# One queue for the key weights, one for x: the first loads of an attention and gMLP block on one core

## The chip, the core and the metric

The kernel runs on one core of a Trainium2 chip. The core has five engines with an instruction stream each: TensorE (PE in the profile), VectorE (DVE), ScalarE (ACT), GpSimd (POOL) and SyncE (SP). SyncE computes nothing here; it issues transfers. ScalarE can issue transfers too, and in this kernel it issues a few. The metric is the time of one execution on the device in microseconds, lower is better; a comparison takes the median of several runs.

## The reference, cut to what matters

Two blocks in a row on x (2048 tokens by 512 features, bf16), each behind a layer norm and with a residual:

```python
x = A_x
h  = x + A(layernorm(x), wqkv, wo)           # linear attention, 32 heads of 16
h2 = h + B(layernorm(h), w_in, w_sp, b_sp, w_out)

# A: phi(t) = where(t > 0, t + 1, exp(t)) + 1e-6
q, k, v = split(x @ wqkv)
kv  = einsum('bhsd,bhse->bhde', phi(k), v);  z = phi(k).sum(s)
out = (phi(q) @ kv) / (phi(q) @ z + 1e-6) @ wo

# B: z1, z2 = halves of gelu(x @ w_in), each 896 wide
g   = w_sp @ layernorm(z2) + b_sp            # w_sp is 2048 x 2048
out = (z1 * g) @ w_out
```

## The kernel before, in words

Tokens are handled in 16 tiles of 128 rows, numbered 0 to 15, and in 4 token groups (tg) of 512. The work runs in these stages, which overlap.

**Loads.** `first_load` and `load_x` issue the first transfers in a fixed chain for each queue. x0 to x3 are one tile each; x4, x6, ... x14 are two tiles each. A load with `behind` waits, on its engine, for another load to land.

**Key units** (`k_unit(n)`, tiles n and n+1). For each tile: statistics (`stats`: a 676 ns `bn_stats`, L511, and a short `bn_aggr`, L512, on VectorE; for the tiles in `ACTS`, two ScalarE passes with accumulation and four GpSimd operations); 1/sqrt(var + eps) (`rstd_act` by Ln and Exp on ScalarE for tiles 0, 2 and 3, `rstd` by pow on GpSimd for others); the norm to `xn` (L556 on VectorE up to tile 5, an Identity on ScalarE from tile 6); the transpose to `xnT` (on TensorE, L570, with a copy by ScalarE up to tile 5; by a DMA transpose on SyncE's queue, named xt6 to xt15, L435, from tile 6); four matmuls with the key weights (L402, `psum<-wqkv,xnT`); `phi` to `pk`; and four matmuls that add pk^T xn into four PSUM banks (L655). Those banks hold a 512 x 512 sum ct, from which the kv product is made later with the value weights `wv` (L720).

**phi** is an Exp on ScalarE from PSUM to `e`, a minimum and an addition on VectorE (L582), and then one of two forms: on VectorE alone a max of (psum + 1 + eps) and e (L587), or, with `split`, an Identity with bias on ScalarE from PSUM to the destination and a max of that and e on VectorE (L585).

**Query units** make phi(q) in `pqT`, from the weights `wq`. **z** is summed with a matmul of ones (L676). Then the kv product (L720), masked to blocks on VectorE (`kvm`), is multiplied by `wo` to `m`; the denominators of a token group (L751) become 1/den by Ln and Exp on ScalarE (`r`, `rcp`), and four copies on SyncE's queue spread that to 128 rows (`r<-rcp`, L742), with which VectorE divides `pqT` (L764).

**h.** For each tile four matmuls `psum<-m,pqT`, and VectorE adds x (L776). Three PSUM banks are used in turn. ScalarE squares h with accumulation (`sh`), GpSimd makes mean and 1/std, VectorE the norm `hn` (L556), and SyncE's queue transposes it to `hnT` (L435, ht0 to ht15).

**The gMLP half.** z2 of a tile is eight matmuls (L802, L805, "psum<-win,hnT"), z1 of a group four (L402). Then w_sp (transposed by DMA on SyncE's queue, `dma_t`, in blocks of 128 columns of the result, whole or as two halves), the gating, and the output product. TensorE's part of this lasts from 64.85 us to the end.

**What sets the order.** Every operation is recorded by `add` with the regions it reads and writes; `ORDER`, a packed list, gives the order of all 961 operations. `schedule` unpacks it and `emit` splits it by engine and puts a semaphore wait in front of an operation that needs another engine or a DMA. Engines run their lists strictly in order, so an operation that waits holds all behind it. A transfer that SyncE issues stands in SyncE's list like any operation. `soft` entries and `cost`, `lat` figures serve the planning only.

**The head's queues before.** SyncE: x0, x2, half of the key weights (wk0), x4, x6 (both behind x2's landing), x8, x10, x12, x14 (behind wk0's), wq, one whole block of w_sp, then xt7, xt6 and on. ScalarE: x1, x3, the other half of the key weights (wk2), then the load of its Exp/Ln table.

Of the kernel before, what the change touches and what calls it, by code (L numbers as in the profile page):

```python
# [8 lines left out]
ACT = mybir.ActivationFunctionType  # L9
ALU = mybir.AluOpType  # L10

P = 128
GRAN = 16
EARLY = 1
SEM_NS = 45.0
ORDER = "c-jTQ17HvU00h8Cwq47%ZQHhO+qGrewr$(CZ5wwH5gAbt9Wf9Su@D<^5Eu2800D@ED2Rr5$b~$}jl4*LqyUHz2nE3iiC_qhWJrz_NQp#9j8w>n{3w9JNQ(-ngvO|hifD@XNQl%(gMui6bjW~0NROh(gp4SL;;4eE$c!dvhAgOttSEtOsEO>Tj&A6I?kI_#D23)|fpBPrmgt4v=!-tcfm*16wy2FdXpPdSi+UJ`GAN7sXn-*oi}6^7B{+=bSc-PYiE=294rqh+XoyA_fPol{e&~-u=!i}@g3dUILzsYxn1sn#foYh6Ay|pf2#+ubi&cn#)i{b{IDz9BieU)ENCaUNMq>@uVLGOw3%X(^W?%v4<1|iU78YVH*5eGG;uKz@fg0)sp5qy2V-AL61U6tJ7GW`VU^_NpGqzwZ=3x)^VkdTCH_qWK_F+E`U@Nxa3a;WjF5n_A;U+HQ8gAh_Zr~N(;5FXjHtypN?&2OEA~+u)1Vi#2BJdF+G7{h8F`nQjKHvvF;uk*QAHLu-zTqprBPPMH49!ps!&o$9Gb*DoGNUja<1-H9G91J6H)1dqQ!@`UGdlA!3-hx8(=aX5F+DRdBQvoaOS2ZqeEfr~EJ*P$$}kwSF*|cGCkwGWb1{GkSeQjvl*L$=3Au#z*pj)~gSA<lCE13Fn3xr~m}Oa?OIe4l*qXiBmVH=}l~|co*p6$smJQgDjaZfK*^@Qcm`&J=eVLTWS%RgQgvq#t$(4dlnUc-9hbgp-TbWvEG@MgdjoUbaBiWA~*pZ#sp99#L138Gxxt%+>f-5<d={22=)L1pSjx(4+d%2HY*p1EDg4LN)sgzl1704hC<zRMaR}SM4Hc=L(Q$~$qCQai^o?%vHQ+DN0PUTiE<y9W#S3VU`K^0aZ713E9VR02z2^CXml~fs(S1Fa%9UkQ|-sKg(;Z>H?6TW2y&EkF@;6bkE25#hNj^S92<4*44A&%#4&f#3H;yg~^ah~9OF63cO;wEn9J>KU7KIBQB;yb?Q2cF}3Uf@OU=4r0xHD2c>HdQk<R|~aND^2DCPUIq1RAp7tA3o(X{$&+a)fawcHHBAeB~u%<RXep;2X#~@bygR3RRn!waD`A!g;Xtl<a6HOO+MlazT_>w;wS!NL|x`<J|+}NRAhbU5B}sY-e!CyP!xqyXh~rdRbgcXD4~8ckrFG3s;h>gD~3KZreZ0!!YP`PDvshRnBr-G`e?9ftFC6Kj%I3zhN_+hs;_2ixVmYIrfQJ7tG{|^l~!w-rYle*HCMybQzO(*qclz%G+MnBr16@ddFrkC8lzd7sC8PPC0eMpO5(Aaqyw6xrCOuOTBh~dsLfiWE!wJs+NPvltP@(U?b@Xk+N71*p}jh+L)xvK+Nb?GqCGmQ<4Wk0I;GP(qeMQY#LnfjI;RvquM4`QD@y5$itl8;rcb)A54x<Yx}&?grJK5^+`g{|O6>#=@JBt;L#6U#J<|(4(Nm@MXT8=drE_{e*B8CiS7q=!z125;*AFFk7XQ*uW%O_T6a7bjmEXZ^!*XbcabAaX2#0lehjSWda#m+{HWzR~M{q<(avn!@WJh-t7jkw-a|{=DKF4t^$8-+obP*SIF_&>!7k3HQbA88kBR6&vH*hmIbxD_ULr-!GH+OlrbSw9A8~1h}w{}IBb|qK#1o!hq_jP{{a67kkdk^#=5AiTp@nBbVIoEInS95jObS>9*M|bu{*Ku8UcMnhTR8MmUZ}Mgj^(+r}Cy(?DPxlsg@np|*kViPsvpvsqJl6}n$V)um3%%G&J<g-u)nmQfqrA+kywYpD*6SSG!F@yV+|!}F)$jF2x7E#KyxJ=~-s`==+q~U7ywkh<AMVe{ZU"


class _Op:
# [233 lines left out]
def bass_sequential_preLN__linear_attn_block__mixer_gmlp__prompt_kernel(  # L253
# [11 lines left out]
    _, S, D = A_x.shape  # L265
    F = B_w_in.shape[1]
    FH = F // 2
    H = 32
# [9 lines left out]
    g = _Prog(nc)  # L278
# [41 lines left out]
    x = g.sbuf("x", o_x, [NT, D], BF16)  # L320
    h = g.sbuf("h", o_x, [NT, D], BF16)
    xn = g.sbuf("xn", o_xn, [NT, D], BF16)
    wqkv = g.sbuf("wqkv", o_wqkv, [KD, 3 * D], BF16)
# [4 lines left out]
    pk = g.sbuf("pk", o_pk, [NT, D], BF16)  # L328
# [146 lines left out]
    def first_load(eng, dst, src, nm, lat, behind=None):  # L475
        q = queue[eng]
        op = load(eng, dst, src, nm, lat)
        op.bias = 1e6
        if q:
            op.soft.add(q[-1].i)  # L480
        if behind is not None:
            op.deps.add(behind.i)
        q.append(op)
        return op

    def load_x(eng, n, w, lat, behind=None):
        return first_load(eng, x[:, n:n + w, :], x_d[n * P:(n + w) * P, :], f"x{n}", lat, behind)

    x0 = load_x("SP", 0, 1, 2150)
    load_x("ACT", 1, 1, 2250)  # L490
    x2 = load_x("SP", 2, 1, 2500)
    load_x("ACT", 3, 1, 2500)
    wk = [first_load(eng, wqkv[:, c:c + 2, D:2 * D], A_wqkv[c * P:(c + 2) * P, D:2 * D], f"wk{c}", 3500)
          for eng, c in (("SP", 0), ("ACT", 2))]
    for n, lat, behind in ((4, 2000, x2), (6, 2200, x2), (8, 1900, wk[0]), (10, 2100, wk[0]), (12, 2300, wk[0]),
                           (14, 2500, wk[0])):
        load_x("SP", n, 2, lat, behind)
    first_load("SP", wqkv[:, :, 0:D], A_wqkv[:, 0:D], "wq", 3400)
    exp_table = g.add("ACT", lambda ac: ac.preload_act_table_set("natural_log_exp_and_others"), [], [], cost=1300)
    exp_table.soft.add(queue["ACT"][-1].i)  # L500
    exps = []
# [12 lines left out]
    def rstd(s, r, n, w, col, neg, sign=1.0):  # L514

        rr, ss = r[:, n:n + w, :], s[:, n:n + w, :]
        pool(lambda p: p.tensor_scalar(rr[:, :, 1:2], ss[:, :, col + 1:col + 2], sign, EPS_LN, op0=ALU.mult,
                                       op1=ALU.add), [ss[:, :, col + 1:col + 2]], [rr], 230)
        pool(lambda p: p.tensor_tensor(rr[:, :, 0:1], rr[:, :, 1:2],  # L519
                                       expo[:, 0:w].rearrange("p (a b) -> p a b", b=1), ALU.pow), [rr, expo], [rr],  # L520
             620 + 120 * (w - 1))
        if neg:
            for i in range(n, n + w):
                pool(lambda p, i=i: p.tensor_scalar(r[:, i, 2:3], s[:, i, col:col + 1], r[:, i, 0:1], -1.0,
                                                    op0=ALU.mult, op1=ALU.mult), [r[:, i, :], s[:, i, :]], [r[:, i, :]], 240)

    def rstd_act(s, r, n, w, col):
        rr, ve = r[:, n:n + w, :], s[:, n:n + w, col + 1:col + 2]
        act_exp(rr[:, :, 1:2], ve, ACT.Ln, 80, bias=epst[:, 1:2], extra=[epst[:, 1:2]])
        act_exp(rr[:, :, 0:1], rr[:, :, 1:2], ACT.Exp, 80, scale=-0.5)  # L530
# [22 lines left out]
    def norm(eng, dst, src, s, r, n, col, w):  # L553
        mean, rst, nmr = s[:, n, col:col + 1], r[:, n, 0:1], r[:, n, 2:3]
        if eng == "DVE":
            return dve(lambda v: v.tensor_scalar(dst, src, mean, rst, op0=ALU.subtract, op1=ALU.mult), [src, mean, rst],  # L556
                [dst], w + 460, acc=4)
        elif eng == "ACT":
            act(dst, src, ACT.Identity, w, bias=nmr, scale=rst, extra=[nmr, rst])
        else:  # L560
            pool(lambda p: p.tensor_scalar(dst, src, rst, nmr, op0=ALU.mult, op1=ALU.add), [src, nmr, rst], [dst],
                 200 + 1.5 * w)
# [43 lines left out]
    def next_pair():  # L606
        pc[0] += 1
        return PAIRS[pc[0] % 2]

    CB, first_xt, second = [4, 5, 6, 7], None, None  # L610
    HEAD, SINGLE = 6, 4
    ACTS = (1,)
    QSPLIT, KSPLIT, CACT = (6, 7), (), 2


    def k_unit(n):
        nonlocal first_xt, second
        b = next_pair()
        for i in (n, n + 1):
            if i in ACTS:  # L620
                s = st[0][:, i, :]
                act(sh_t[0], x[:, i, :], ACT.Identity, D, accum=s[:, 0:1])
                act(sh_t[1], x[:, i, :], ACT.Square, D, scale=D ** -0.5, accum=s[:, 1:2])
                moments(s, 6, D)
                rpow(s[:, 7:8], rs[0][:, i, 0:1])
            else:
                op = stats(x, 0, i)
                if i == 0:
                    second = warmup(16, 60, op)
                if n == 0:  # L630
                    rstd_act(st[0], rs[0], i, 1, 6)
        if n == 2:
            rstd_act(st[0], rs[0], n, 2, 6)
        elif n:
            rstd(st[0], rs[0], n, 2, 6, n >= HEAD)
        for i in (n, n + 1):
            norm("DVE" if n < HEAD else "ACT", xn[:, i, :], x[:, i, :], st[0], rs[0], i, 6, D)
            if n < HEAD:
                pe_transposes(xn[:, i, :], b + i % 2, xnT, i, second)
            else:  # L640
                g.last = dma_t(xnT[:, :, i * P:(i + 1) * P], xn[:, i, :], f"xt{i}")
                if i == HEAD:
                    first_xt = g.last
        for i in (n, n + 1):
            matmuls(bank(b + i % 2), [(xnT[:, c, i * P:(i + 1) * P], wqkv[:, c, D:2 * D]) for c in range(KD)])
        if n < SINGLE:
            for i in (n, n + 1):
                phi(pk[:, i:i + 1, :], b + i % 2, 1)
        else:
            phi(pk[:, n:n + 2, :], b, 2, n in KSPLIT)  # L650

        def fn(pe, i):
            inst = None
            for c in range(KD):
                inst = pe.matmul(bank(CB[c]), lhsT=xn[:, i, c * P:(c + 1) * P], rhs=pk[:, i, :],  # L655
                                 start=i == 0, stop=i == NT - 1)
            return inst
        for i in (n, n + 1):
            PE(lambda pe, i=i: fn(pe, i), [xn[:, i, :], pk[:, i, :]], [bank(b) for b in CB], KD * 216)
# [67 lines left out]
    for c in range(KD):  # L727
        b = CB[1 - c % 2]
# [100 lines left out]
    k = 0  # L829
# [190 lines left out]
```

## Time and profile before

| | us |
|---|---|
| median of 4 runs | 233.42 (232.74 to 233.94) |
| the profiled execution | 233.36 |
| its span in the profile | 231.6 |
| TensorE busy | 224.8 |
| VectorE busy | 161.3 |
| ScalarE busy | 104.7 |
| GpSimd busy | 44.9 |

The granted clock of TensorE is 1.0 in the whole profile. The profile is of one execution; times in it count from the start of the span, and 1.76 us of the execution lie outside it. A line of the timeline gives the start, the length, the engine, the source line, the operation with output and input, the number of instructions merged into it, and, in brackets, how long the engine sat idle before it and what ended that. A matmul's own length (379 ns for 512 columns) includes its way through the array; successive ones start 216 ns apart. A line of DMA issues ends with the time from issue to landing. The chain of waits is followed back from the last instruction, and its shares are 89% TensorE, 4% DMA and 3% ScalarE.

### The profile page before, as it was taken

Reading aid. Unit: us, or ns where it says so; the run is one execution under the profiler, and the core shown is the slowest. Engines: PE = TensorE matmul, PEld = TensorE weight load, DVE = VectorE, ACT = ScalarE, POOL = GpSimd, SP = SyncE. Lnnn points to the kernel's source line nnn. Section 1 sums busy time; section 2 is a strip of 40 time slices with the busy share of each in tenths; the row PEclk is TensorE's granted clock in tenths of the full one; section 3 lists DMA queues with packets and bytes.
Section 4 is the critical chain, followed back from the end, with each engine's and each line's share of the span. In section 5 each row is a group of like instructions: output and inputs, shape, how many; then the busy total and the mean of one; then the engine's idle time right before and its main releaser. Section 6 shows DMA issues by size and latency. Waiting matters only on the chain.

```text
span 231.6 us, 3254 instructions
## 1 busy us (share of the span) xinstructions
PE 224.8 (97%) x1203; PEld 110.5 (48%) x1203; DVE 161.3 (70%) x323; ACT 104.7 (45%) x193; POOL 44.9 (19%) x134
## 2 busy tenths in 40 slices
PE   7898999999999999999999999999999999999995
PEld 7433444453444443454544444444455555555452
DVE  3998656646986650237489989979795566785485
ACT  5794754399889876679862010101021211123010
POOL 2436300000467608033771000000000000000000
PEclk9999999999999999999999999999999999999999
DMA  5893359927457537959999700000000000020025
GB/s 185 260 214 69 67 143 274 343 64 178 96 110 135 115 71 134 190 112 175 181 231 204 159 3 0 0 0 0 3 0 1 0 3 0 21 71 3 0 81 191
DMA packets 58864, 23.68 MB, mean 102 GB/s; under 512 B 48480, under 2 KB 58720, under 8 KB 58848
## 3 DMA queue, kind: packets, MB, share of 16 engines
q1 hardware_dynamic: 58144, 22.88, 44.5%
q10 hardware_dynamic: 704, 0.59, 0.7%
q8 instruction: 9, 0.15, 0.2%
q14 instruction: 7, 0.06, 0.1%
HBM read 7.47 MB, written 2.10 MB: 41 GB/s over the span
## 4 chain that ended last, share of the span: by engine, by line
PE 89%; DMA 4%; ACT 3%; DVE 1%; issue 1%
PE psum L402 72%; PE psum L802 6%; PE psum L655 5%; PE psum L805 4%; DMA xnT<-xn 2%; DMA hnT<-hn 1%; DMA x<-in_A_x_dram 1%; DVE st L511 1%; ACT sh L421 1%; ACT xn L421 1%; PE psum L570 1%; ACT e L421 1%; ACT xnT L421 0%; PE psum L751 0%; PE psum L676 0%
## 5 line engine op out<-in xcount | busy, mean ns | idle before, releaser
L421 ACT ACTIVATE psum<-psum 128x256 f32<-128x256 f32 (+1 forms) x33 | 14.3, 445 | 90.8 <-PE psum L402 63.1
L402 PE MATMUL psum<-wsp,z 128*128 128x512 bf16 x208 | 47.7, 379 | 0.0
L402 PEld LDWEIGHTS psum<-wsp,z 128*128 128x128 bf16 x208 | 20.4, 98 | 22.9
L402 PE MATMUL psum<-hnT,win 128*128 128x512 bf16 x112 | 26.1, 379 | 0.0
L421 ACT ACTIVATE e<-psum 128x1024 bf16<-128x1024 f32 (+1 forms) x18 | 16.7, 926 | 15.0 <-PE psum L402 14.4
L402 PE MATMUL psum<-t,s 128*128 128x512 bf16 x96 | 22.4, 379 | 0.0
L421 ACT ACTIVATE z1T<-psum 128x512 bf16<-128x512 f32 x28 | 16.6, 594 | 4.9 <-PE psum L402 4.8
L802 PE MATMUL psum<-win,hnT 128*128 128x512 bf16 x64 | 16.4, 379 | 0.5 <-DMA hnT<-hn 0.5
L402 PE MATMUL psum<-wout,z1T 128*128 128x256 bf16 (+1 forms) x83 | 16.7, 315 | 0.0
L402 PEld LDWEIGHTS psum<-hnT,win 128*128 128x128 bf16 x112 | 10.0, 98 | 13.2 <-ACT z1T L421 3.8
L402 PE MATMUL psum<-wqkv,xnT 128*128 128x512 bf16 x64 | 15.0, 379 | 1.2 <-DMA xnT<-xn 1.2
L421 ACT ACTIVATE z<-psum 128x896 bf16<-128x896 f32 x16 | 14.6, 910 | 2.9 <-PE psum L805 2.8
L402 PE MATMUL psum<-xnT,wqkv 128*128 128x512 bf16 x64 | 15.6, 379 | 0.0
L655 PE MATMUL psum<-pk,xn 128*128 128x512 bf16 x64 | 15.3, 379 | 0.0
L402 PE MATMUL psum<-m,pqT 128*128 128x512 bf16 x64 | 14.8, 379 | 0.2 <-DVE h L776 0.2
L402 PEld LDWEIGHTS psum<-t,s 128*128 128x128 bf16 x96 | 9.4, 98 | 10.3
L776 DVE SCALAR_TENSOR_TENSOR h<-psum,x 128x512 bf16<-128x512 f32 x16 | 10.8, 687 | 4.8 <-PE psum L402 4.8
L582 DVE TENSOR_SCALAR e<-e 128x1024 bf16<-128x1024 bf16 (+1 forms) x18 | 7.0, 391 | 9.2 <-ACT e L421 9.0
L805 PE MATMUL psum<-win,hnT 128*128 128x384 bf16 x64 | 13.0, 326 | 0.0
L924 DVE TENSOR_TENSOR u<-psum,bsp 128x512 bf16<-128x512 f32 x16 | 11.0, 687 | 2.8 <-PE psum L402 2.7
L556 DVE TENSOR_SCALAR z<-z,st,rs 128x896 bf16<-128x896 bf16 x16 | 7.2, 494 | 7.3 <-POOL rs L519 7.3
L511 DVE BATCH_NORM_STATS2 st<-x 128x6 f32<-128x512 bf16 x15 | 9.7, 676 | 3.5 <-DMA x<-in_A_x_dram 3.5
(113 smaller groups left out, 347.5 us busy)
## 6 DMA issues: line engine op xcount, KB each, us to landing
r<-rcp SPq DMA_DIRECT2D x16, 128.0 KB, 2.7
out_dram<-h SPq DMA_DIRECT2D x15, 128.0 KB, 1.8
win<-in_B_w_in_dram SPq DMA_DIRECT2D x2, 896.0 KB, 6.7
x<-in_A_x_dram SPq DMA_DIRECT2D x6, 256.0 KB, 3.4
wqkv<-in_A_wqkv_dram SPq DMA_DIRECT2D x2, 512.0 KB, 5.1
wout<-in_B_w_out_dram SPq DMA_DIRECT2D x1, 896.0 KB, 6.2
wo<-in_A_wo_dram SPq DMA_DIRECT2D x1, 512.0 KB, 8.4
bsp<-in_B_b_sp_dram SPq DMA_DIRECT2D x1, 512.0 KB, 5.7
```

Of the source, the lines that this page charges most:

```text
L402: inst = pe.matmul(out_ap, lhsT=a, rhs=b, start=start and i == 0, stop=stop and i == len(pairs) - 1, **kw)
L421: return g.add("ACT", lambda ac: ac.activation(out_ap, in_ap, func, **kw), [in_ap, *extra], [out_ap] + ([accum] if accum is not None else []),
L511: dve(lambda v: v.bn_stats(s[:, 0:6], src[:, n, :]), [src[:, n, :]], [s[:, 0:6]], D)
L556: return dve(lambda v: v.tensor_scalar(dst, src, mean, rst, op0=ALU.subtract, op1=ALU.mult), [src, mean, rst], [dst], w + 460, acc=4)
L570: inst = pe.transpose(tv[:, c * P:(c + 1) * P], src[:, c * P:(c + 1) * P], ident)
L582: dve(lambda v: v.tensor_scalar(e, e, 1.0, EPS_PHI, op0=ALU.min, op1=ALU.add), [e], [e], w * GW, acc=4)
L655: inst = pe.matmul(bank(CB[c]), lhsT=xn[:, i, c * P:(c + 1) * P], rhs=pk[:, i, :], start=i == 0, stop=i == NT - 1)
L776: dve(lambda v, n=n, b=b, s=s: v.scalar_tensor_tensor(h[:, n, :], bank(b), 1.0, x[:, n, :], op0=ALU.mult, op1=ALU.add, accum_out=s[:, 0:1] ...
L802: pe.matmul(bank(b), lhsT=hnT[:, c, n * P:(n + 1) * P], rhs=win2[:, c, 0:GW], start=c == 0, stop=c == KD - 1)
L805: inst = pe.matmul(bank(b + 1, F2), lhsT=hnT[:, c, n * P:(n + 1) * P], rhs=win2[:, c, GW:FH], start=c == 0, stop=c == KD - 1)
L924: dve(lambda v: v.tensor_tensor(t, bank(b), add, ALU.add), [bank(b), add], [t], GW, ps=True)
```

## The change

The first loads are dealt out anew. ScalarE's queue carries one load only, all four row blocks of the key weights (512 KB) in one transfer. SyncE's queue carries every x load: x0, x1, x2, x3, then x4 and x6 behind x2's landing, the rest behind that of the key weights, then wq. `EARLY = 0` takes away the whole block of w_sp that was transposed at the head; that block is now transposed in two halves, later. `ACTS = ()` gives tile 1's statistics to VectorE and its 1/std to ScalarE's Ln and Exp. `KSPLIT = (0, 1)` makes phi of key tiles 0 and 1 the split form, with an Identity on ScalarE. `ORDER` is new as a whole: the order of nearly every engine's list differs from before. `ND` and `LEAD` are empty and do nothing.

In the new order TensorE transposes tiles 0 to 2, does the key matmuls of tile 0, transposes tile 3, and goes on with the key matmuls of tiles 1 to 3; VectorE does the statistics of tiles 0 to 3 before any norm. SyncE's list is x0 to x14, wq, nine xnT transposes, wout, the last xnT transpose, win2, half a block of w_sp, wo, wv, win1, the r copies of groups 0 and 1, the other half block, the r copies of group 2, ht0, ht1 and on; before, wv stood ahead of the last xnT transpose, wout and two half blocks of w_sp followed, then win1, win2 and wo, and no w_sp stood among the r copies of groups 0 to 2.

```diff
-EARLY = 1
+EARLY = 0
...
-    x0 = load_x("SP", 0, 1, 2150)
-    load_x("ACT", 1, 1, 2250)
-    x2 = load_x("SP", 2, 1, 2500)
-    load_x("ACT", 3, 1, 2500)
-    wk = [first_load(eng, wqkv[:, c:c + 2, D:2 * D], A_wqkv[c * P:(c + 2) * P, D:2 * D], f"wk{c}", 3500)
-          for eng, c in (("SP", 0), ("ACT", 2))]
-    for n, lat, behind in ((4, 2000, x2), (6, 2200, x2), (8, 1900, wk[0]), (10, 2100, wk[0]), (12, 2300, wk[0]),
-                           (14, 2500, wk[0])):
+    wk = first_load("ACT", wqkv[:, :, D:2 * D], A_wqkv[:, D:2 * D], "wk", 4300)
+    load_x("SP", 0, 1, 2250)
+    load_x("SP", 1, 1, 2350)
+    x2 = load_x("SP", 2, 1, 2550)
+    load_x("SP", 3, 1, 2750)
+    for n, lat, behind in ((4, 1750, x2), (6, 1950, x2), (8, 2000, wk), (10, 2200, wk), (12, 2400, wk), (14, 2600, wk)):
         load_x("SP", n, 2, lat, behind)
...
-    ACTS = (1,)
-    QSPLIT, KSPLIT, CACT = (6, 7), (), 2
+    ACTS, ND, LEAD, lead = (), (), 0, []
+    QSPLIT, KSPLIT, CACT = (6, 7), (0, 1), 2
...
-                phi(pk[:, i:i + 1, :], b + i % 2, 1)
+                phi(pk[:, i:i + 1, :], b + i % 2, 1, i in KSPLIT)
```

## The prediction

> **What bounds the kernel now.** I read the shares first, then the chain of work that ended last, then TensorE's idle times in the timeline, then SyncE's issues and the landings.
>
> Busy time by engine, from the page:
>
> ```profile
> PE 224.8 (97%) x1203; PEld 110.5 (48%) x1203; DVE 161.3 (70%) x323; ACT 104.7 (45%) x193; POOL 44.9 (19%) x134
> ```
>
> TensorE (PE) is busy for all but 6.8 us. The change neither adds nor removes a matmul, so only those 6.8 us can move. The timeline of TensorE (start, length, what, idle before) names the idle time that matters:
>
> ```profile
> 14.42 2.75 PE L655 MATMUL psum<-pk,xn 128*128 128x512 bf16 x12
> 18.33 1.90 PE L402 MATMUL psum<-wqkv,xnT 128*128 128x512 bf16 x8 [1.16 <-DMA xnT<-xn]
> ...
> 55.06 0.39 PE L402 MATMUL psum<-wo,kvm 128*128 128x512 bf16 x1 [0.31 <-ACT m L421]
> ...
> 63.02 1.04 PE L402 MATMUL psum<-m,pqT 128*128 128x512 bf16 x4 [0.23 <-DVE h L776]
> 63.99 0.40 PE L751 MATMUL psum<-pqT,zc 128*32 128x512 bf16 x4
> 64.85 1.04 PE L802 MATMUL psum<-win,hnT 128*128 128x512 bf16 x4 [0.46 <-DMA hnT<-hn]
> ```
>
> After 64.85 no idle of TensorE is listed to the end. So the last 231.60 - 64.85 = 166.75 us are fixed work, and **the sum is about one number: when the first L802 matmul starts.** The chain of waits says what leads there:
>
> ```profile
> 14.36 3.92 DMA xnT<-xn
> 18.28 0.04 issue
> 18.33 1.90 PE psum L402 x8
> ...
> 61.33 3.47 DMA hnT<-hn
> 64.80 0.05 issue
> 64.85 1.04 PE psum L802 x4
> ```
>
> SyncE's issues say why the transpose that ends at 18.28 began only at 14.36:
>
> ```profile
> 8.99 5.31 SPq L435 DMA_TRANSPOSE wsp<-in_B_w_sp_dram  x1
> 14.36 5.54 SPq L435 DMA_TRANSPOSE xnT<-xn  x4
> ```
>
> The w_sp transpose holds the queue for 5.31 us. ScalarE had finished the first tile that the queue was to transpose (12.20 + 0.80) at 13.0.
>
> **The change part by part.** *The w_sp transpose leaves the head.* The first xnT transpose can issue as soon as ScalarE writes its tile, and its landing falls from 3.9 us to the 2.5 of the median row. If nothing else changed, TensorE would go on at 17.0 (12 matmuls of 0.216 from 14.42) instead of 18.33, a gain of 1.3 at most. What is late next is TensorE's own work before it, so the loads must be counted.
>
> *The loads.* Before, x0 and x1 go out at 0.79 and 0.80 on two queues, x2 and x3 behind them, and one half of the key weights on each. These rows carry the landings (count, KB each, us to landing):
>
> ```profile
> x<-in_A_x_dram SPq DMA_DIRECT2D x2, 128.0 KB, 2.7
> x<-in_A_x_dram ACTq DMA_DIRECT2D x2, 128.0 KB, 2.9
> wqkv<-in_A_wqkv_dram SPq DMA_DIRECT2D x1, 256.0 KB, 4.8
> wqkv<-in_A_wqkv_dram ACTq DMA_DIRECT2D x1, 256.0 KB, 5.0
> ```
>
> x0 keeps 3.47. x1 takes the place of x2 as SyncE's second load: 1.25 + 2.8 = 4.05. x2 and x3 are third and fourth, and no row shows that. From below: the second tile lands 0.56 after the first, so 4.6 and 5.2. From above: SyncE's third and fourth 128 KB were the weight half, 1.71 + 4.8 = 6.5, so 5.3 and 6.5. I take 4.8 and 5.5, nearer to the spacing, as x rows lie next to each other in memory and the weights' do not. The whole weight load lands between those ends, at 6.0 to 6.7, ahead of its use.
>
> At one place a rule speaks against this part. In 2.5 to 3.5 us the two queues' recorded packets are 217 and 179, near equal. The Trainium skill, "DMA: Bandwidth & Descriptors", "Issuing engines are not separate DMA queues" and "Queues, rings and completion order", says that both queues run on the same 16 engines, taking turns, and that a second issuer saves only issue time. By it the four tiles would advance only as fast as the weights beside them and x3 would land with the weights: the second rival's 233.5, where the rows' spacing gives 232.8.
>
> VectorE then does stats of four tiles (tile 1 moves here from ScalarE, which drops two ACTIVATEs of 0.63; GpSimd drops four operations): x1 4.08 to 4.7, x2 4.85 to 5.5, x3 5.55 to 6.2, aggregates to 6.4 (before 5.79). The pair's Ln and Exp take 0.6 to 7.05; xn0 and xn1 fill 6.4 to 7.05; xn2 and xn3 start at 7.07 and 7.4. Transposes of tiles 0 to 2 run 6.86 to 7.85 and the first key matmul starts at **7.95, before 7.75.** Four groups (0.86 each) and tile 3's transposes (0.32) end at 11.7.
>
> *phi of tiles 0 and 1.* ScalarE gains two Identity passes, which the trace lacks at this size: half of the 128x1024 row (1.11) is 0.55, the 128x512 copy 0.60. VectorE's 0.67 (PSUM source) becomes a max at 0.42 at most (128x512 bf16 row). ScalarE holds them: from 7.3 to 11.8 it does 4 copies, 2 exps and 2 Identities, 8 x 0.5. Were that cover gone, the copy of tile 3's transpose would be late and TensorE would wait 0.5. For VectorE it is 0.25 less, twice, ahead of the two later tiles' norms.
>
> *To the 18.33 line.* Transposes of tiles 4 and 5 end at 12.4 (before 12.7), then four pk and two key groups, 6 x 0.86, to **17.6**. xn7 is ready at 13.5, its transpose lands at 13.55 + 2.5 to 2.9 = 16.4, the next 1.26 later: both in time. So 17.6 for 18.33, a gain of 0.7.
>
> *The middle.* The order is written anew. The last pk groups end at 46.3 (before 47.03). ScalarE's chain from ct to the last m is the same 13 instructions; with one 0.5 wait for TensorE it ends at 55.7, and h starts at 55.75 (before 56.58). But h of tile 0 on VectorE now stands behind the minimum of the last query exp: exp 55.7 to 56.6, minimum to 57.05, h 57.1 to 57.8 (before 57.65 to 58.3). Square, GpSimd's four operations and the norm take what they took (57.65 to 61.3), so hn0 ends at 60.75; SyncE is free then (r from 57.85, four at 0.62). It issues at 60.78 and the landing takes its 3.47: 64.25, so **L802 starts at 64.3, before 64.85.** TensorE itself is ready at 63.45: from 55.75 eight h groups of 0.86, one L751 group of 0.33, and a 0.5 wait, since tile 4's products need tg 1's division, which VectorE does between h tiles.
>
> *w_sp elsewhere.* The head's block is now two halves, one behind win2 and one between the r copies of groups 1 and 2; the other fourteen follow among and behind the hnT transposes. Issue is 1.31 to 2.77 each. Nine of them stand behind the last hnT, near 97.5: at 1.35 they are issued by 110 and land within 6, before TensorE's first use at 120.15. wv stands behind wout, win2, one half and wo: about 3.1 MB from 31.5 at the 247 GB/s that those loads made before (4.3 MB, 31.05 to 48.5) is 44.2, needed at 48.5. Cost nothing; the cover is 4 us of TensorE's q and z groups, and without it TensorE would wait at the kv product.
>
> **Sum:** 64.85 - 64.3 = 0.55, so 233.36 (the profiled execution: span 231.60 and 1.76 around it) - 0.55 = 232.8. The median of the four runs, 233.42, is 0.06 above it, so the forecast for a median is 232.8 too.
>
> **Rivals.** *Both stalls shrink fully.* If hnT lands in the 2.5 us of its median row, L802 starts at 63.45, where TensorE is ready: 1.4 gained, 232.0; with x3 at 5.2 (0.3 more) 231.7. For it: the 3.47 had r copies around it. Against: they still are.
>
> *The change does not do what it says.* x3 lands with the weights at 6.5: everything to 17.6 moves by 0.7 to 18.3, and since the h chain hangs on the same start, L802 is at 65.0: 233.5, no change.
>
> *Slower: the w_sp half between the r copies.* It is issued at 55.5 and all r copies of group 2 and hnT stand behind it on SyncE's queue. Its landing is 3.7 us in one row, 6.5 in a row behind wout, 8.9 in the head row (a whole one):
>
> ```profile
> wsp<-in_B_w_sp_dram SPq DMA_TRANSPOSE x1, 3.7
> ...
> wsp<-in_B_w_sp_dram SPq DMA_TRANSPOSE x1, 6.5
> ...
> wsp<-in_B_w_sp_dram SPq DMA_TRANSPOSE x1, 8.9
> ```
>
> At 3.7 it is gone by 59.2. From 7 us on it decides: hnT lands no sooner than about 2 us after it. At 8.9: 64.4 + 2.5 = 66.9, L802 2.1 later than before, 235.5. Against it: the queue holds only small copies at 55.5, as in the 3.7 row.
>
> **How the numbers follow.** Forecast 232.8: 0.50, its own range 232.3 to 233.3. Full shrink: 0.25. No change: 0.12. Slower: 0.13. Low end 231.6, the first rival with the early x3 and 0.1 of scatter; high end 234.3, the slower case up to a landing of 7.7; what is beyond, and what lies below, is under 0.2. A measurement of this kernel tells about 0.5%, 1.17 us, from no change: under 232.25 is faster, over 234.59 slower. Faster takes the first rival and a little of the forecast, 0.28; slower takes most of its case, 0.12; the rest, 0.60, is within.
>
> **What would show it.** Right: no w_sp transpose on SyncE before 30 us; x3's stats at 5.4 to 5.8; the first key matmul near 7.95; the wait before 18 gone with those matmuls at 17.6; L802 near 64.3 still ended by hnT; nothing idle after it. Wrong: x3's stats after 6.3, an idle before the transposes of tile 4 or 5, hnT's landing far from 3.5, a wait for wv near 49, or any idle after 65, where a new order could make one that I price at nothing.

## The result and the profile after

The changed kernel takes 234.60 us (median of 44 runs, 233.71 to 235.77), the kernel before 233.66 in the runs beside it (63 runs, 232.29 to 235.79). The ratio is 1.0042 with a 95% interval of 1.0032 to 1.0053: slower by 0.94 us. The forecast was 232.8, and the median lies 0.3 above the top of the range. The profiled execution of the changed kernel took 234.23 us with a span of 232.5.

The page's line of busy times, to set beside that of before:

```profile
PE 226.9 (98%) x1203; PEld 112.9 (49%) x1203; DVE 161.7 (70%) x325; ACT 103.5 (45%) x193; POOL 43.1 (19%) x130
```

TensorE has the same 1203 matmuls and is busy for 2.1 us more. No more work was done; some of it ran at a lower clock. The chain of waits in the head of the changed kernel (start, length, what) shows where:

```profile
1.25 4.07 DMA x<-in_A_x_dram
5.32 0.02 issue
5.35 0.69 DVE st L509
6.04 0.09 DVE st L510
6.13 0.05 issue
6.18 1.89 PE psum L592 x16
8.07 1.32 PE psum L568 x12
9.39 1.46 PE psum L402 x4
10.85 0.22 PE psum L568 x4
11.08 2.59 PE psum L402 x12
```

The chain begins with x1, which needs 4.07 us to land. Behind it stand tile 1's statistics, and behind those, on VectorE, tile 0's short aggregation (L510), for which the second warm-up batch on TensorE waits (L592: matmuls on zeros that write nothing of use). That batch takes 1.89 us for 16 matmuls of 128 columns, the first four key matmuls 1.46; the same key matmuls later take 2.59 for 12, which is 0.86 for four. TensorE ran at half speed there. Its timeline has the idle time ahead of the second batch, and the end of the stall that the change was to remove:

```profile
1.04 3.81 PE L592 MATMUL psum<-warm 128*128 128x128 bf16 x34 [1.04 <-POOL warm L439]
6.18 1.89 PE L592 MATMUL psum<-warm 128*128 128x128 bf16 x16 [1.33 <-DVE st L510]
7.93 1.46 PE L568 MATMUL psum<-ident,xn 128*128 128x128 bf16 x12
9.22 1.63 PE L402 MATMUL psum<-wqkv,xnT 128*128 128x512 bf16 x4
...
17.44 1.89 PE L658 MATMUL psum<-pk,xn 128*128 128x512 bf16 x8
19.16 1.89 PE L402 MATMUL psum<-wqkv,xnT 128*128 128x512 bf16 x8
```

In the last line there is no bracket: the wait of 1.16 us for the first transposed copies is gone. Yet these matmuls start at 19.16, not at 18.33 as before; the first key matmul starts at 9.22, not at 7.75. The middle and the end of the kernel:

```profile
63.28 1.90 PE L402 MATMUL psum<-m,pqT 128*128 128x512 bf16 x8 [0.30 <-DVE h L779]
65.11 0.40 PE L754 MATMUL psum<-pqT,zc 128*32 128x512 bf16 x4
65.66 1.04 PE L805 MATMUL psum<-win,hnT 128*128 128x512 bf16 x4
```

The first z2 matmul (L805, L802 before) starts at 65.66 instead of 64.85. From there to the end of the span it is 166.8 us, as before (166.75). So 0.8 of the 0.87 us between the two profiled executions is already there at 19.16 us, and the head has to explain it.

The loads come from the table of DMA issues (KB each, median us to landing):

```profile
x<-in_A_x_dram SPq DMA_DIRECT2D x4, 128.0 KB, 3.9
wqkv<-in_A_wqkv_dram ACTq DMA_DIRECT2D x1, 512.0 KB, 4.2
```

A tile of 128 KB and a weight load of 512 KB need nearly the same time. One by one, issued and landed: x0 0.79 and 3.23, the keys 0.79 and 4.98, x1 1.25 and 5.32, x2 1.72 and 5.70, x3 2.18 and 6.02. The three tiles follow the keys at 0.32 to 0.38 us each. The packets recorded between 3.00 and 4.25 us say the same (queue, packets, MB, share of the 16 engines; q10 carries ScalarE's issues and q1 SyncE's):

```profile
q10 hardware_dynamic: 404, 0.41, 97.2%
q1 hardware_dynamic: 1, 0.00, 0.2%
```

x1 had been issued since 1.25, and while the keys moved nothing of it did.

### The profile page after: what moved, and what is told of

It is laid out like the page before. It is cut to its first block, busy times and chain, and to the rows that moved or that the text cites. A ratio compares the mean times of both kernels' runs of the same rounds, so it can differ in the third digit from the quotient of the medians.

```text
span 232.5 us, 3248 instructions
## 1 busy us (share of the span) xinstructions
PE 226.9 (98%) x1203; PEld 112.9 (49%) x1203; DVE 161.7 (70%) x325; ACT 103.5 (45%) x193; POOL 43.1 (19%) x130
## 4 chain that ended last, share of the span: by engine, by line
PE 90%; DMA 3%; ACT 3%; DVE 1%; POOL 1%; issue 1%; SPq 0%
PE psum L402 71%; PE psum L805 6%; PE psum L658 6%; PE psum L808 4%; DMA x<-in_A_x_dram 2%; DMA hnT<-hn 1%; PE psum L568 1%; ACT m L421 1%; PE psum L592 1%; ACT r L421 1%; ACT e L421 1%; ACT rcp L421 0%; PE psum L723 0%; PE psum L679 0%; PE psum L688 0%
## 5 line engine op out<-in xcount | busy, mean ns | idle before, releaser
L821 DVE BATCH_NORM_STATS2 st<-z 128x6 f32<-128x512 bf16 x9 | 6.1, 693 | 17.2 <-ACT z L421 17.1
L805 PE MATMUL psum<-win,hnT 128*128 128x512 bf16 x64 | 16.4, 379 | 0.1
L402 PE MATMUL psum<-wqkv,xnT 128*128 128x512 bf16 x64 | 15.9, 390 | 0.0
L509 DVE BATCH_NORM_STATS2 st<-x 128x6 f32<-128x512 bf16 x16 | 10.4, 678 | 4.7 <-DMA x<-in_A_x_dram 4.7
L928 DVE TENSOR_TENSOR z1T<-u,z1T 128x512 bf16<-128x512 bf16 x28 | 11.5, 420 | 0.5
```

The lines of the kernel that those rows point to most:

```text
L402: inst = pe.matmul(out_ap, lhsT=a, rhs=b, start=start and i == 0, stop=stop and i == len(pairs) - 1, **kw)
L509: dve(lambda v: v.bn_stats(s[:, 0:6], src[:, n, :]), [src[:, n, :]], [s[:, 0:6]], D)
L805: pe.matmul(bank(b), lhsT=hnT[:, c, n * P:(n + 1) * P], rhs=win2[:, c, 0:GW], start=c == 0, stop=c == KD - 1)
L821: dve(lambda v, n=n, s=s: v.bn_stats(s[:, 0:6], z2[:, n, 0:GW]), [z2[:, n, 0:GW]], [s[:, 0:6]], GW)
L928: dve(lambda v: v.tensor_tensor(z, t, z, ALU.mult), [t, z], [z], GW, acc=2)
```

## The experiments

**The theory.** (1) The key load is issued ahead of x1 to x3 and is served ahead of them, though it stands in another queue; x1 is late by it. (2) The gap that this leaves in TensorE's work keeps or brings TensorE to half clock for some microseconds. (3) The w_sp part is worth what the removed stall cost, or more. **Rivals:** four tiles on one queue come late by themselves; the clock comes up at a moment that has nothing to do with the gap; phi, the statistics, or the new order of the later instructions cost the time.

A number is needed below that the profile does not print: the mean granted clock of each timed execution. The changed kernel's 44 executions fall in two groups, 24 at 0.992 or 0.993 with a median of 234.81 us and 20 at 0.999 or 1.0 with 234.08. Of 112 executions of the kernel before in the series below, one was at 0.993. (One stretch of 3.41 us at half speed takes 0.7% off the mean.) A mean of 1.0 doesn't say that the head ran at full speed, as the record of the clock can begin late: the profiled execution of the changed kernel has 1.000, its record begins at 10.46, and its matmuls run at half speed up to there.

### Key load behind ScalarE's table load

```diff
-    exp_table.soft.add(queue["ACT"][-1].i)
+    wk.soft.add(exp_table.i)
```

> The changed kernel with one exchange: ScalarE loads its function table first and issues the key weights after it (about 2.1 us instead of 0.79), so that x0 to x3 are issued ahead of the keys. Theory (the key load, issued before x1, is moved ahead of x1 to x3): x1 lands at 3.6-4.1 instead of 5.32, x3 by 4.8, the keys at 6.0-6.7; the first key matmul at 7.5-8.2 instead of 9.22, the matmuls behind the first transposed copies (19.33) at 17.5-18.0, and the time 232.5-233.4. Rival (x1 to x3 are late because the four x loads stand in one queue, whatever ScalarE's queue does): x1 still lands after 4.9 and the time stays at 234.3-234.9.

Measured: 234.54 us, ratio 1.0031 (1.0013 to 1.0049). The edit did not do what it was for, as ScalarE's timeline shows:

```profile
0.79 1.28 ACT L497 ACT_TABLE_LOAD   x1 [0.79 <-PEq L1008]
0.82 0.45 ACTq L432 DMA_DIRECT2D wqkv<-in_A_wqkv_dram  x1
```

The key load is issued 0.03 us after the table load begins, not after it ends. x1 landed at 5.20. So this is the changed kernel again, within its scatter (7 of 12 executions at 0.992 or 0.993), and decides nothing between the theories.

### x1 and x3 on ScalarE's queue again

```diff
-    wk = first_load("ACT", wqkv[:, :, D:2 * D], A_wqkv[:, D:2 * D], "wk", 4300)
+    wk = load("ACT", wqkv[:, :, D:2 * D], A_wqkv[:, D:2 * D], "wk", 4300)
...
-    load_x("SP", 1, 1, 2350)
+    load_x("ACT", 1, 1, 2350)
...
-    load_x("SP", 3, 1, 2750)
+    load_x("ACT", 3, 1, 2750)
+    wk.soft.add(queue["ACT"][-1].i)
...
-    exp_table.soft.add(queue["ACT"][-1].i)
+    exp_table.soft.add(wk.i)
```

> The changed kernel with only its load part undone: x1 and x3 on ScalarE's queue ahead of the key weights (still one load), x0 and x2 on SyncE's; no w_sp at the head, phi and the statistics as changed. Theory (all the loss comes from the keys that pass ahead of x1 to x3, and the w_sp part is worth 1.2 to 1.5): x1 lands at 3.6-3.9, x3 by 4.5, the keys at 6.3-6.8, the first key matmul at 7.3-7.9; mean clock 1.0 or 0.999 in every execution; the time 231.8-232.6. Rival (phi on ScalarE, tile 1's statistics on VectorE or the other order of the later transfers cost something too): landings as above, but 232.8-233.6.

Measured: 233.01 us, ratio 0.9983 (0.9968 to 0.9997); x1 landed at 3.75, x3 at 4.33, the keys at 6.50; no execution of 12 below 0.999. The landings are the theory's, the time is the rival's: 1.6 us better than the changed kernel, but 0.9 worse than the kernel before with the w_sp part alone (below). Something else in the change costs.

### Keys last of the five on SyncE's queue

```diff
-    wk = first_load("ACT", wqkv[:, :, D:2 * D], A_wqkv[:, D:2 * D], "wk", 4300)
+    wk = load("SP", wqkv[:, :, D:2 * D], A_wqkv[:, D:2 * D], "wk", 4300)
...
-    load_x("SP", 3, 1, 2750)
+    wk.soft.add(load_x("SP", 3, 1, 2750).i)
...
-    exp_table.soft.add(queue["ACT"][-1].i)
```

> The changed kernel with the key load moved from ScalarE's queue to SyncE's, issued behind x0 to x3 (about 2.6 us). The four x tiles stay on one queue as in the changed kernel. Theory (the key load ahead of x1 in time is what delays it): x1 lands at 3.5-4.2, x3 by 4.9, the keys at 6.3-7.1, and the time is 231.8-232.8. Rival (four x tiles on one queue come late by themselves): x1 at 4.9 or later, the time 234.0-235.0.

Measured: 232.91 us, ratio 0.9982 (0.9968 to 0.9997); x1 landed at 3.28, x2 at 4.34, x3 at 4.73, the keys at 6.31; 0 of 12 at 0.993. The rival is out: the four tiles share one queue as in the changed kernel, and are early. What made them late is the key load that was issued before them. The matmuls behind the first transposed copies in this kernel:

```profile
16.83 0.81 PE L657 MATMUL psum<-pk,xn 128*128 128x512 bf16 x2
17.48 1.89 PE L402 MATMUL psum<-wqkv,xnT 128*128 128x512 bf16 x8
```

17.48 without a wait is 0.1 from the prediction's 17.6, and 232.9 is 0.1 from its 232.8 (and 0.1 above the theory's range). So the prediction's time fits this kernel, from which the changed kernel differs in when the keys are issued. In part that is luck: x1 and x3 landed 0.8 us earlier than it had reckoned (4.05 and 5.5), and TensorE then idled for 0.26 us before 11.72 and 0.13 before 14.88, which it had not counted.

### The load part alone, in the kernel before

```diff
-    load_x("ACT", 1, 1, 2250)
+    load_x("SP", 1, 1, 2250)
...
-    load_x("ACT", 3, 1, 2500)
+    load_x("SP", 3, 1, 2500)
-          for eng, c in (("SP", 0), ("ACT", 2))]
+          for eng, c in (("ACT", 0), ("ACT", 2))]
```

> The kernel before with the loads alone changed: x0 to x3 on SyncE's queue, both halves of the key weights on ScalarE's; the w_sp block stays at the head. Theory (keys issued at 0.8 and 1.3 pass ahead of x1 to x3): x1 lands at 4.6-5.4 instead of 3.67 and the first key matmul is 0.7 to 1.5 later than 7.75, but the wait for the first transposed copies (1.2 us) takes up most of it: 233.6-234.2. Rival (x1 to x3 aren't held back by the key load): x1 lands at 3.9-4.2 and the time is 233.2-233.6, with the keys a little later.

Measured: 234.32 us, ratio 1.0027 (1.0011 to 1.0043), 0.1 above the theory's range, 9 of 12 executions at 0.993. TensorE idles for 0.95 and 0.32 us ahead of the first transposes here. x1 landed at 4.25, outside the theory's 4.6 to 5.4 and just past the rival's band. The single landings tell why: issued at 0.79 (x0), 0.79 (first key half), 1.25 (x1), 1.28 (second half), 1.71 (x2), 2.18 (x3), they landed at 2.99, 3.84, 4.25, 4.96, 5.32 and 5.69. That is the order of issue over both queues: x1 had only the first half in front of it, x2 and x3 had both. In VectorE's timeline the statistics of x0 are done and the wait is for x2 (in the changed kernel it was for x1):

```profile
3.75 0.18 DVE L512 BATCH_NORM_AGGREGATE st<-st 128x2 f32<-128x6 f32 x1
5.34 1.29 DVE L511 BATCH_NORM_STATS2 st<-x 128x6 f32<-128x512 bf16 x2 [1.41 <-DMA x<-in_A_x_dram]
```

### The w_sp part alone, in the kernel before

```diff
-EARLY = 1
+EARLY = 0
```

The block's two halves take the places of the next two, and so on; the rest of SyncE's list keeps its order.

> The kernel before with the w_sp part of the change alone: no w_sp transpose among the head loads, its block in two halves at the places of later halves. Theory (the first transposed copies waited 1.2 us for the queue behind that block): they land by 17, the key matmuls behind them start at 17.0-17.4 instead of 18.33, and the time is 232.1-232.8. Rival (xn6 and xn7 from ScalarE or their statistics are late next and take the wait's place): the matmuls start after 18.0 and the time is 233.3-233.8.

Measured: 232.07 us (6 runs), ratio 0.9927 (0.9907 to 0.9947): 1.5 us faster than the kernel before, and the fastest of all versions. xt7 landed at 16.36, xt6 at 17.67, and the matmuls that had waited start at 17.83 without a wait, not at the 17.0 to 17.4 of the theory, as TensorE idled for 0.56 us ahead of the transposes at 12.09 (TensorE's timeline):

```profile
16.75 1.24 PE L655 MATMUL psum<-pk,xn 128*128 128x512 bf16 x5
17.83 1.46 PE L402 MATMUL psum<-wqkv,xnT 128*128 128x512 bf16 x6
```

In the profiled execution (232.52 us, the slowest of the six) only 0.5 of the gain is won here. Another 0.5 is won where the first hnT lands, 3.00 us behind its issue instead of 3.47. Why it landed sooner is open; that time lies between 2.4 and 4.4 in the profiles of the kernels here, with no pattern that the experiments settle. So the 1.5 us in the median are measured, but only a third of them is traced to the removed wait.

### Tile 0's aggregation ahead of tile 1's statistics

The edit is in `ORDER`; in words, for VectorE's list:

```diff
-VectorE: bn_stats x0, bn_stats x1, bn_aggr x0, bn_stats x2
+VectorE: bn_stats x0, bn_aggr x0, bn_stats x1, bn_stats x2
```

> The changed kernel with two instructions of VectorE exchanged: the aggregation of tile 0 before the statistics of tile 1, so that the second warm-up batch no longer waits for x1. Loads as in the changed kernel. Theory (TensorE's idle 1.33 us at 4.85 to 6.18 keeps its clock low until 10.5): the second batch follows the first at about 4.85 without a gap, matmuls are at full speed by 7, the first transposes take 0.055 us each instead of 0.107, the first key group 0.86 instead of 1.46, and the time is 233.5-233.9, that is 0.7 to 1.1 less than the changed kernel's. Rival (the clock comes up at a moment that this gap doesn't set): transposes still at 0.107 us, a gain of 0.3 at most from the earlier end of the batch, 234.2-234.7.

Measured: 234.79 us, ratio 1.0038 (1.0021 to 1.0054). The median speaks against the theory and the profile for it, and both have the same reason. The profiled execution took 233.57 us and is one of only two of 12 at 0.999; in its timeline of TensorE the batch follows without a gap and all after it is at full speed:

```profile
1.04 5.41 PE L592 MATMUL psum<-warm 128*128 128x128 bf16 x50 [1.04 <-POOL warm L439]
7.80 1.12 PE L568 MATMUL psum<-ident,xn 128*128 128x128 bf16 x12 [1.34 <-DVE xn L554]
8.88 1.04 PE L402 MATMUL psum<-wqkv,xnT 128*128 128x512 bf16 x4
```

But the gap has only moved: TensorE is now idle for 1.34 us after the batch, as x1 is late all the same. In the other 10 executions the mean clock is 0.992 or 0.993, and they take 234.85 (median). One profile was the lucky case, and only the spread of the timed runs showed it.

### The gap covered

```diff
-VectorE: bn_stats x0, bn_stats x1, bn_aggr x0, bn_stats x2
+VectorE: bn_stats x0, bn_aggr x0, bn_stats x1, bn_stats x2
...
-                    second = warmup(16, 60, op)
+                    second = warmup(32, 60, op)
```

> The changed kernel with tile 0's aggregation ahead of tile 1's statistics on VectorE and 32 instead of 16 matmuls in the second warm-up batch, so that TensorE runs on from 1.04 to about 7.2-8.3 and has next to no gap before the first transposes at 7.8. In the changed kernel 24 of 44 executions had a mean clock of 0.992 or 0.993 and were about 0.8 us longer than those at 1.0; with the aggregation first alone it was 10 of 12. Theory (the gap in TensorE's work ahead of the transposes costs a stretch at half clock in those executions): at most 2 of 12 at 0.993, median 233.4-233.9. Rival (the dip comes whenever the loads are late, whatever TensorE does before): half or more at 0.993, median 234.4-235.0.

Measured: 233.70 us (233.52 to 233.95), ratio 1.0002 (0.9982 to 1.0021), 0 of 12 executions at 0.993. x1 still landed at 5.39. With the loads as late as in the changed kernel, sixteen more matmuls on zeros win 0.9 us, since they leave no gap in TensorE's timeline:

```profile
1.04 6.56 PE L592 MATMUL psum<-warm 128*128 128x128 bf16 x66 [1.04 <-POOL warm L439]
7.93 1.12 PE L568 MATMUL psum<-ident,xn 128*128 128x128 bf16 x12 [0.33 <-DVE xn L554]
```

The idle time is 0.33 us instead of 1.33, and the 12 transposes take 1.12 instead of 1.46.

### A gap made, with the loads in time

The kernel before with the w_sp part, and

```diff
-                    second = warmup(16, 60, op)
+                    second = warmup(1, 60, op)
```

> The kernel before with the w_sp part alone (232.07 us), and 1 matmul instead of 16 in its second warm-up batch: loads unchanged, TensorE idle from about 4.9 to 6.3. Theory (such a gap costs a stretch at half clock): some executions, a third or more of 12, at a mean clock of 0.993 and 0.6-1.3 us longer; median 232.2-233.3. Rival (the gap is harmless, the dip belongs to late loads): every execution at 1.0 or 0.999 and the time 231.9-232.3.

Measured: 233.38 us, ratio 0.9990 (0.9973 to 1.0007), that is 1.3 more than with 16 matmuls and 0.1 above the theory's range; 7 of 12 executions at 0.993 (median 233.51), the others 232.85. The profiled one is at 0.993. Its stretches (length, then busy us and instructions of PE, PEld, DVE, ACT and POOL; granted clock, DMA share, GB/s):

```profile
4.94:8.35 3.41, 1.70 (x19) 1.14 (x20) 3.02 (x10) 2.71 (x9) 1.37 (x4) 1.00 0.75 245
8.35:11.76 3.41, 3.41 (x10) 1.19 (x9) 3.22 (x12) 2.02 (x4) 1.70 (x4) 0.50 0.92 284
```

TensorE was busy for half of the first stretch, and the next 3.41 us ran at half the clock, although TensorE was then busy all the time. The loads were early here, so the rival is out: the gap does it.

### The changed kernel once more

> The changed kernel once more, for a trace of an execution with a mean clock of 0.993 (24 of its 44 executions). Theory, if it is one: the clock record shows one stretch of about 3.4 us at half speed that begins between 6 and 10 us, behind TensorE's gap at 4.85 to 6.18, and the matmuls in it are spaced as at half speed; time 234.4-235.4. If it is one of the others: the clock comes up for good between 5 and 11 us, 233.7-234.5. Rival to both: the dip lies elsewhere in the kernel, away from the head.

Measured: 234.56 us, 5 of 8 executions at 0.992 or 0.993, and the profiled one (234.49) is among them. The kernel is unchanged; its stretches, with the same columns:

```profile
4.24:7.65 3.41, 1.45 (x22) 1.10 (x20) 2.34 (x8) 0.91 (x5) 0.00 (x0) 1.00 0.51 157
7.65:11.07 3.42, 3.18 (x18) 1.99 (x19) 3.42 (x10) 2.00 (x5) 0.61 (x2) 0.50 0.94 316
```

This is the same picture in the changed kernel itself. The stretch at half clock begins at 7.65, right before the first transposes. In the first profile of the changed kernel the slow matmuls reach from the start to 10.46: both ways the transposes and the first key matmuls run at half speed.

### phi alone, the statistics alone

Both on the kernel before with the w_sp part (232.07).

```diff
-    QSPLIT, KSPLIT, CACT = (6, 7), (), 2
+    QSPLIT, KSPLIT, CACT = (6, 7), (0, 1), 2
...
-                phi(pk[:, i:i + 1, :], b + i % 2, 1)
+                phi(pk[:, i:i + 1, :], b + i % 2, 1, i in KSPLIT)
```

> The kernel before with the w_sp part alone (232.07 us) and with the phi part: head tiles 0 and 1 get 1+x from ScalarE and the maximum on VectorE from SBUF. Theory (both engines have room here; TensorE has next to no idle time behind the head): within 0.15 of it, 231.9-232.3. Rival (ScalarE, which then copies the later transposes and normalizes tiles 6 and 7, becomes late): the key matmuls behind the first transposed copies start at 18.1 or later instead of 17.83 and the time is 232.4-233.0.

Measured: 232.25 us, ratio 0.9937 (0.9916 to 0.9958), against 0.9927 (0.9907 to 0.9947) without it: no difference that can be told.

```diff
-    ACTS = (1,)
+    ACTS = ()
```

> The kernel before with the w_sp part (232.07 us) and the statistics part: tile 1's mean and variance on VectorE, its Ln and Exp on ScalarE, instead of two accumulating passes on ScalarE and four GpSimd operations; loads as before. Theory (no loss from this part when x1 is in time): the first key matmul at 7.7-8.2 as there (7.91) and 231.8-232.4. Rival (one more statistics pass on VectorE ahead of x2's and x3's delays xn0 to xn3 by its 0.6): first key matmul at 8.4 or later, 232.5-233.0.

Measured: 232.52 us, ratio 0.9950 (0.9932 to 0.9968), first key matmul at 8.44 instead of 7.91. Both numbers are the rival's, at its low end: xn0 stands behind one more statistics pass. But the interval overlaps that of the kernel without this part, so 0 to 0.5 us is all that can be said of the time.

This run also shows a gap of nearly the same length that cost no clock:

```profile
6.93 0.40 PE L570 MATMUL psum<-ident,xn 128*128 128x128 bf16 x4 [1.28 <-DVE xn L556]
...
8.44 3.62 PE L402 MATMUL psum<-wqkv,xnT 128*128 128x512 bf16 x16
```

The 16 key matmuls behind it take 3.62 us, as at full speed in the kernel before, and none of the six executions is at 0.993. In the 3.41 us around that gap TensorE was busy for 1.81 us, against 1.45 and 1.70 in the two stretches above that were followed by half clock. Whether the line runs between these is not shown: the load part alone lost clock in 9 of 12 executions with shorter gaps in its profile.

### The remaining half microsecond

With the keys behind x the changed kernel takes 232.91, the kernel before with the w_sp part 232.07. Five runs looked for the difference. All loads on SyncE's queue in the latter:

```diff
-    load_x("ACT", 1, 1, 2250)
+    load_x("SP", 1, 1, 2250)
...
-    load_x("ACT", 3, 1, 2500)
+    load_x("SP", 3, 1, 2500)
-          for eng, c in (("SP", 0), ("ACT", 2))]
+          for eng, c in (("SP", 0), ("SP", 2))]
```

> The kernel before with the w_sp part (232.07 us) and all head loads on SyncE's queue: x0, x1, x2, x3, then the two halves of the key weights, then the rest. Theory (what matters is that the keys are issued behind the x tiles, not which queue carries them): x1 lands by 3.5, x3 by 4.8, the keys by 6.8; the wait of 0.56 us for x4 and x5 shrinks; the time 231.6-232.1, the best of all. Rival (one queue for everything delays the second key half past 7.3): the first key matmul after 8.3 and 232.3-232.8.

Measured: 232.59 us, ratio 0.9956 (0.9937 to 0.9974); x1 landed at 3.41, x3 at 4.62, the keys at 6.27, first key matmul at 7.96. It is no gain over two queues; the time is the rival's, though its cause did not occur.

The half w_sp block among the r copies, which was the prediction's slower case:

```diff
-SyncE: r copies of groups 0 and 1, w_sp half, r copies of group 2, ht0
+SyncE: r copies of groups 0 and 1, r copies of group 2, ht0
```

> The changed kernel with the key load behind x0 to x3 on SyncE (232.91 us), and the second half of the first w_sp block taken from between the r copies (issued at 55.65, 1.38 us long) to its successor's place, behind the seventh hnT transpose. Theory (that half isn't what delays the first hnT: its issue waits for hn0): hnT lands within 0.2 of before and the time is 232.6-233.1. Rival, the prediction's slower case (the half between the copies holds up r and with it h and hnT): the first z2 matmul 0.4 or more earlier and 232.0-232.5.

Measured: 233.07 us, ratio 0.9972 (0.9959 to 0.9986). The first z2 matmul came no earlier: 8.72 us behind the first m,pqT matmul, against 8.49. The half costs nothing where it stands.

All parts of the change but the early key load, in the order of the kernel before (all loads on SyncE's queue as in the diff above, and):

```diff
-EARLY = 1
+EARLY = 0
...
-    ACTS = (1,)
-    QSPLIT, KSPLIT, CACT = (6, 7), (), 2
+    ACTS = ()
+    QSPLIT, KSPLIT, CACT = (6, 7), (0, 1), 2
...
-                phi(pk[:, i:i + 1, :], b + i % 2, 1)
+                phi(pk[:, i:i + 1, :], b + i % 2, 1, i in KSPLIT)
```

> All parts of the change but the early key load, in the order of the kernel before: w_sp off the head, tile 1's statistics on VectorE, phi of head tiles 0 and 1 on ScalarE, x0 to x3 and then both key halves on SyncE. It computes what the changed kernel with the keys behind x on SyncE (232.91) does, and differs from it in the order of the later instructions alone. Theory (the order written for the middle of the changed kernel costs 0.5 to 0.8): the stretch from the first m,pqT matmul to the first win,hnT matmul is 7.7-7.9 as in the other kernels with the order of before, not 8.5, and the time is 231.9-232.5. Rival (the parts together cost it, in the head): the stretch may be short, but the key matmuls behind the first transposed copies start after 17.9 and the time is 232.7-233.2.

Measured: 232.50 us, ratio 0.9947 (0.9931 to 0.9962), against 0.9982 and 0.9972 for the same parts in the new order: in the medians the new order costs 0.4 to 0.6 us. They differ in one thing more, the keys being two loads here and one there, which no run separates. Nor do the profiles say where the time goes: the stretch was 8.33, not 7.7 to 7.9, as hnT took 3.53 to land, and the first z2 matmul started at 64.05, against 64.15 with the keys on SyncE. What differs in every profile is the start of hn0, counted from the first m,pqT matmul of the stretch: 4.30 or 4.31 us in all eight profiles of kernels with the order of before, 4.86 or 4.87 in seven of the new order (without the two next ones, which change it, and the one with the long warm-up batch, 5.12). The second of GpSimd's operations ahead of hn0 in the timeline, first with the new order (keys on SyncE), then with the order of before:

```profile
58.76 0.75 POOL L534 TENSOR_SCALAR st<-st 128x1 f32<-128x1 f32 x1
```
```profile
58.70 0.31 POOL L536 TENSOR_SCALAR st<-st 128x1 f32<-128x1 f32 x1
```

It is the same operation, and takes 0.44 us longer in the new order, where VectorE does a product of pqT and r (58.65 to 59.34) beside it. To try whether that is what costs the time, the product was moved, in the kernel with the keys on SyncE, behind hn0 and then behind the third h:

```diff
-VectorE: h0, product, h1, product, h2, hn0
+VectorE: h0, product, h1, h2, hn0, product
```

> The changed kernel with the key load behind x0 to x3 on SyncE (232.91 us), and one more exchange: on VectorE the product pqT by r that stood between the second and third h goes behind the first hn. The stretch from the first matmul of the attention output (m,pqT) to the first of z2 (win,hnT) took 8.49 us there and 7.79 in the kernel before with the w_sp part alone; a GpSimd operation in it took 0.75 us instead of 0.31 while that product ran. Theory (that overlap makes hn0 and its transpose 0.4 late, and this is most of what separates the two kernels): the GpSimd operation back at 0.31, the stretch 8.0-8.2, the time 232.4-232.7. Rival (the landing of hnT is set elsewhere, by the queue behind r): the stretch stays at 8.4 or more and the time at 232.8-233.2.

```diff
-VectorE: h0, product, h1, product, h2, hn0
+VectorE: h0, product, h1, h2, product, hn0
```

> The changed kernel with the key load behind x0 to x3 on SyncE (232.91 us), with the product pqT by r exchanged with the third h alone (in the trial before this it went behind hn0, which was 0.42 earlier, but TensorE then waited 1.87 us for the product). Theory (the GpSimd operation that ran beside the product costs the first hnT 0.4): GpSimd's second operation at 0.31, hn0 at most 4.5 us behind the first matmul of the stretch (4.86 there), TensorE's wait for the product below 0.5, the time 232.4-232.8. Rival (the stretch is set by how long the transposed copy takes to land, and hn0 earlier by 0.4 is used up there or by the product): 232.8-233.3.

Measured: 233.61 us (ratio 0.9999, 0.9985 to 1.0012) and 233.36 us (0.9978, 0.9965 to 0.9990). Neither gains. In the first the operation is back at 0.31 and hn0 0.42 earlier, but TensorE waits 1.87 us for the product. In the second the operation is at 0.31 and the next one, a power, at 0.91 instead of 0.57, beside the moved product; TensorE waits 0.72 for it. So the new order goes with about half a microsecond, and hn0 is 0.56 late in it; that the one slow GpSimd operation is the cause was tried and not shown, and the cause stays open.

## Why the prediction was wrong

The steps in the order of the working:

- **Which number counts: right.** Behind the first z2 matmul there are 166.8 us, as counted.
- **w_sp off the head: right.** The wait is gone; alone this part is worth 1.5 us in the median, though in its profile the wait gives only 0.5 of that, and 0.5 more comes from an hnT landing that nothing explains. This is the gain that the rest of the change gave back, and 0.9 more.
- **The loads: wrong, and this is the step that failed.** "x1 takes the place of x2 as SyncE's second load: 1.25 + 2.8 = 4.05." It landed at 5.32. The 2.8 came from a kernel in which nothing but tiles was issued ahead of that tile; here 512 KB were. The whole key load was expected at 6.0 to 6.7 and came at 4.98, ahead of x1. What the runs show in its place: loads are served in the order of issue, over both queues. The clue lay in the trace of before, where two tiles and then one key half were issued on each queue and landed in that order; the equal packet counts of the two queues, read as turns between them, were just as much a picture of that, as each pair of loads was issued within 0.01 us. By the trial with the gap covered, the lateness alone costs 0.6 to 0.8 us (233.70 against 232.91 to 233.07).
- **The Trainium skill's rule** ("DMA: Bandwidth & Descriptors", "Issuing engines are not separate DMA queues") was right that a second issuer brings no second path. By taking turns ("Queues, rings and completion order") x3 was to land with the keys at 6.5; it landed at 6.02, and the keys 1.04 us before it. No turns are seen between the keys and x1: from 3.00 to 4.25 us, 404 of the 405 packets were the keys'.
- **The clock: not in the working at all.** The prediction took every duration at full speed, so that half clock in the head was a term put at nothing ("only those 6.8 us can move", but TensorE's busy time itself grew by 2.1), and did not follow the second warm-up batch, which hangs on tile 0's aggregation and so, in the new order of VectorE, on x1. This costs 0.9 us in the median (234.60 against 233.70 with the gap covered), at least as much as the lateness itself.
- **phi: right**, no cost. **Statistics:** 0 to 0.5, where 0.2 was expected in the first key matmul from the loads and the statistics together.
- **The middle: right in sum, by luck in its parts.** From the key matmuls behind the transposed copies to the first z2 matmul 46.7 us were predicted (17.6 to 64.3), 46.5 measured. hn0 stood 0.3 later in it than worked out, and an hnT landing of 2.96 instead of 3.47 made up for it.
- **wv and the w_sp halves: right**, no cost; nothing waits for them (wv landed at 46.49, not 44.2, still ahead of its use), and TensorE has no idle time behind the first z2 matmul.
- **The rivals.** "x3 lands with the weights" had 233.5 and stood on the right doubt; it missed that the keys would pass the tiles, and it too knew only the full clock. The slower case had times on both sides of the measured one, but by luck: its half block was issued at 57.34 and landed at 60.89, ahead of the first hnT's issue at 62.65, and moving it gained nothing.

The versions in a row give the sum: 233.66 before, 232.07 with the w_sp part, 232.50 with the other parts in the old order, 232.91 to 233.07 in the new order, 233.70 with the keys ahead of x and TensorE kept busy, 234.60 with the gap. These are medians of several series, each good to about 0.2.

## What to carry to other kernels

A load on an idle queue isn't free: in these runs what was issued first was served first, whichever engine issued it, so issue the bytes that the first instruction needs before the many that come later. If a change makes TensorE wait in its first microseconds, price the clock as well as the wait, and try to cover the gap with work that needs no data. Where a profile is much better or worse than the median of the runs, look at how the runs split before reading a theory out of it.

## What the runs showed of the hardware

- **Order of service of loads.** In six issues over two queues the landings came in the order of issue (issued at 0.79, 0.79, 1.25, 1.28, 1.71, 2.18, landed at 2.99, 3.84, 4.25, 4.96, 5.32, 5.69).
- **A short gap can cost clock.** Stretches of 3.41 us in which TensorE was busy for 1.45 and 1.70 us were each followed by 3.41 us at half clock; one with 1.81 us was not. The Trainium skill ("TensorE: Matmul & The Clock Gate", "What's actually happening") has the window of 3413 ns, and that it runs free of the kernel's start. That fits what the two profiles of one kernel show, full clock at 4.24 and half again at 7.65 in one, full clock first at 10.46 in the other; a mean clock of 1.0 alone doesn't tell whether the clock came up early and stayed, or late. The page speaks of an idle window of about 3.4 us before the clock falls; here single idle times of 1.33 and 1.51 us, with 0.3 to 0.5 more in the same stretch, were enough.
- **A table load does not hold back a transfer** that ScalarE issues behind it: 0.82 us for the issue, 0.79 to 2.07 for the table.
- **GpSimd operations on single columns** took 0.75 instead of 0.31, and 0.91 instead of 0.57, while VectorE multiplied bf16 tiles of 128x1024 beside them.
